# Stores of finished output tiles issued by SyncE in place of ScalarE, with a new table of priorities

## The chip, the cores and the metric

The kernel runs on one core of one Trainium2 chip. The metric is device time in microseconds (us) of one execution; lower is better. A core has TensorE (PE, with its weight loads shown apart as PEld), VectorE (DVE), ScalarE (ACT), GpSimd (POOL) and SyncE (SP). Each engine takes its own instructions in a fixed order and waits on semaphores for the others. In this program SP and ACT issue the transfers (DMAs) between HBM and the on-chip memory; everything that PE produces lies in eight PSUM banks until ACT or DVE copies it out.

## The reference

Two layers follow each other. The first is attention over 8 batches and 8 heads: 512 local tokens with a window of 32 tokens on either side, and 32 global tokens that see everything. The second takes its output as `x` (8 x 544 tokens that are kept, 512 wide), sends each token through the two best of four experts, and each expert is a causal attention with heads of 64.

```python
s_g  = scale * q_g @ k_all.T ; out_g = softmax(s_g) @ v_all            # 32 global tokens
s_l  = concat(scale * q_l @ k_g.T, where(|i-j|<=32, scale * q_l @ k_l.T, -1e9))
out_l = softmax(s_l) @ concat(v_g, v_l)                                # 512 local tokens
logits = x @ w_gate ; topk = two largest of 4 ; w = softmax over the two
for e in range(4):
    q, k, v = x @ wq[e], x @ wk[e], x @ wv[e]
    a = softmax(causal(scale * q @ k.T))
    out += (e in topk) * w[e] * (a @ v @ wo[e])
```

## The kernel before

The work is cut into steps. A step is one pair of heads of one batch of the first layer (32 pairs), and beside it a quarter of the second layer for a batch that is some steps behind. For one pair, `p1_load` and `p1_load_values` fetch `kn`, `qn` and `v` (line 407, SP), `p1_trans` turns them, `p1_scores` multiplies (32 calls that the profile shows as 64 matmuls, L681), `p1_softmax` runs on DVE and ACT (L693, L696), `p1_ptrans` turns the result (L714), `p1_av` multiplies with `v` (64 matmuls, L744). `long_scores` (L816, L824), `p1_global_av` (40 matmuls, L882) and `m_tail_av` (L1204) serve the global tokens. The second layer has `m_qk` (L912) and `m_v` (L943), 12 long matmuls each, `m_scores` (L1065), `m_softmax` (L1080 DVE, L1084 ACT, L1100 POOL), `m_ptrans` (turns, L714, then copies `ptu` and `ptl` out of PSUM), `m_av` (L1150) and the output.

The output is made by `out_tile`. It does six matmuls into a PSUM bank (L1223), has ACT copy the bank into an `ot` tile (L390; there are three `ot` buffers, which the loads of the next batch's global tokens use as well), and issues the store (L1230). `m_out` calls it for the four tiles of 128 tokens of a batch. Tiles 0 and 1 have their rows in mirrored groups and need four stores of 32 rows each; their stores go to SP. Tiles 2 and 3 need one store of 128 rows; their stores go to ACT. `m_out_tail` calls it once for batches 0 to 3 and once for batches 4 to 7, for the 32 global tokens of four batches at a time, with four stores of 32 rows; the first of these two goes to ACT by the default `via="ACT"`. The last batch and the second tail have `last` set, and either SP or ACT takes each of their stores.

The order is not written out by hand. Every piece of work is recorded by `op` with an estimated cost, and `Plan.place` then places all of them on the five engines by those estimates. Among what is ready on an engine the lowest `prio` goes first; `prio` is 100 per step plus small offsets. The table `SHIFT` (line 88) adds an offset of up to 150 to single pieces, found by kind, cost and step. So a changed table, or a piece on another engine, can change the order everywhere. What comes out is a fixed order per engine. Transfers report their landing on eight semaphores that the program uses in turn, for SP and ACT alike, in the order in which the planner emitted the transfers; before an issue the queue waits until the earlier transfer on the same semaphore has landed.

Of the kernel before, what the change touches and what calls it, by code (L numbers as in the profile page):

```python
# [49 lines left out]
class Op:  # L50
    def __init__(self, k, engs, ns, fn, prio, packets, shape, slow, code, flow):
# [34 lines left out]

OWN = 100
SHIFT = {
    "evac": {(180, 101): -100, (266, 110): 30, (276, 115): 100, (276, 123): 80, (369, 140): -110,
        (448, 103): 40, (475, 100): 130, (475, 102): 120, (475, 103): 90, (475, 106): 10, (475, 116): 80},  # L90
    "high_low": {(264, 125): 70, (332, 108): 100, (332, 109): -70, (332, 113): -50, (332, 114): 100,
        (332, 120): 20, (332, 125): 40, (477, 123): 30, (598, 119): 120, (598, 121): 70},
    "load": {(550, 104): 80, (550, 106): -10, (550, 108): -110, (550, 109): 100, (550, 111): 150,
        (550, 115): 110},
    "long_scores": {(60, 105): 80, (60, 129): -150, (60, 139): -110, (80, 115): -120, (80, 127): 10,
        (880, 103): -60, (880, 107): -70, (880, 109): -40, (880, 119): -40, (880, 125): -150, (880, 139): -120},
    "m_av": {(2220, 111): 30, (2220, 115): 90, (2220, 123): 40, (2220, 131): -10},
    "m_gates": {(350, 106): -40, (350, 123): -20, (630, 123): 140},
    "m_qk": {(1504, 107): 150, (1504, 112): -40, (1504, 124): 40, (1504, 136): 120},
    "m_scores": {(431, 110): 50, (431, 112): 50, (431, 116): 120, (431, 120): 90, (431, 124): 80,  # L100
# [3 lines left out]
    "m_softmax": {(80, 111): 60, (80, 119): 100, (211, 109): 80, (211, 121): -40, (344, 118): -90,  # L104
        (344, 126): -40, (344, 130): -70, (386, 131): -150, (386, 139): 50, (477, 109): -50, (477, 119): -90,
        (477, 125): 40, (599, 125): -70, (610, 108): 20, (644, 139): 20, (705, 114): 60},
    "m_tail_av": {(583, 113): -150, (583, 117): 40, (583, 125): 80, (583, 133): -90},
    "m_tail_factor": {(480, 123): 130},
    "m_tail_softmax": {(610, 119): -40, (745, 119): 30},
    "m_v": {(1440, 118): -40, (1440, 122): -30},  # L110
    "m_v_tails": {(330, 119): -150, (1062, 127): 90},
    "out_tile": {(450, 125): 70, (1400, 113): 90, (1400, 137): 150, (1400, 141): 150},
# [20 lines left out]
    "setup_masks": {(700, 105): 150},  # L133
    "turn_halves": {(250, 108): 20, (250, 109): -30, (250, 110): 120, (250, 118): -20, (250, 119): 20,
# [5 lines left out]
    "turned": {(84, 103): 150, (84, 109): 90, (84, 111): 10, (84, 113): 90, (84, 115): 100, (84, 123): 120,  # L140
        (220, 103): 140, (220, 113): -50, (255, 107): 90, (255, 113): 80, (255, 117): 120, (255, 131): 150},
}


# [193 lines left out]
def fused_kernel(ctx: ExitStack, tc: tile.TileContext, q_l, k_l, v_l, q_g, k_g, v_g,  # L338
# [552 lines left out]
    M = {}  # L891
# [158 lines left out]
    MIRRORED = (0, 1)  # L1050
# [161 lines left out]
                              ((lambda: y[0].t[:, :, b % 4, :], (y[0], b % 4)),  # L1212
                               (lambda: y[1].t[:, :, b % 4, :], (y[1], b % 4))), [(sm, 6)])

    def out_tile(y, lhs, dsts, via="ACT", last=False):

        hi, lo = weights["o"]
        po = ps([128, DM], "po")
# [14 lines left out]
    def m_out(b, i):  # L1233
        y = [(t, (c, n0)) for t in M[b, "yo"] for c in range(2) for n0 in ((0, 256) if b == B - 1 and c == 1 else (0,))
             if n0 == 0 and (i > 1 or n0 == 0 and not (b == B - 1 and c == 1)) or n0 == 256 and i < 2]
        at = Y_AT[i]
        if i in MIRRORED:
            dsts = [(out[b, 128 * i + 96 - 32 * g:128 * i + 128 - 32 * g, :], slice(32 * g, 32 * g + 32)) for g in range(4)]
        else:
            dsts = [(out[b, 128 * i:128 * i + 128, :], slice(0, 128))]  # L1240
        out_tile(y, lambda part, c: M[b, "yo"][part].t[:, c, at:at + 128], dsts, "SP" if i in MIRRORED else "ACT",
                 b == B - 1)

    def m_out_tail(g):
# [182 lines left out]
```

## Time and profile before

| | before |
|---|---|
| median of 3 runs | 467.47 us (467.24, 467.47, 469.96) |
| the profiled execution's own time | 469.88 us |
| its span, first to last instruction | 468.1 us |
| PE busy | 448.4 us (96%) |
| DVE, ACT, POOL busy | 377.2, 325.3, 289.8 us |
| stores of `ot` issued by SP, by ACT | 62, 26 |
| mean granted TensorE clock | 0.996 |

The profile is of one execution. Busy time is the union of an engine's instructions; a queue's waits and its issuing of transfers don't count as busy and are shown with a q (SPq, ACTq). A wait is put down to what ended last before it. The clock is given as a share of full speed: 1.0 is 2.4 GHz and 0.5 is 1.2 GHz.

### The profile page before, as it was taken

How to read it: one execution, taken by the hardware profiler on the slowest of the kernel's cores; microseconds unless marked ns; L12 is line 12 of the kernel's file. 1: busy time of each engine (PE TensorE's matmuls, PEld its weight loads, DVE VectorE, ACT ScalarE, POOL GpSimd, SP SyncE). 2: the span in 40 equal slices, each digit the busy share in tenths (PEclk: the TensorE clock that was granted, in tenths of full speed). 3: DMA queues.
4: the chain of work that ended last, by engine and by line, in shares of the span. 5: the costliest groups of instructions: out<-in, count | busy, mean ns of one | idle time of the engine just before them, and what ended most of it. 6: DMA issues, size and time to landing. Idle time of an engine off the chain costs nothing.

```text
span 468.1 us, 24864 instructions
## 1 busy us (share of the span) xinstructions
PE 448.4 (96%) x10124; PEld 389.1 (83%) x10124; DVE 377.2 (81%) x1689; ACT 325.3 (69%) x1166; POOL 289.8 (62%) x563
## 2 busy tenths in 40 slices
PE   8867999999999999999999999969999999999996
PEld 6656988897879988888979988858998899889875
DVE  6987899999887996789977997938977788568662
ACT  4886588886677776777766777937767666646481
POOL 8978878987987298722678693585849133232420
PEclk9999999999999999999999999999999999999999
DMA  8698566766526255432527424472022000200033
GB/s 179 136 188 150 110 121 118 154 104 119 100 56 144 50 110 105 114 65 49 107 44 171 88 54 71 107 153 64 5 56 74 22 4 3 63 32 1 4 92 113
DMA packets 182387, 40.95 MB, mean 87 GB/s; under 512 B 177664, under 2 KB 177664, under 8 KB 182272
## 3 DMA queue, kind: packets, MB, share of 16 engines
q1 hardware_dynamic: 179488, 34.51, 37.7%
q10 hardware_dynamic: 2784, 4.85, 3.0%
q8 instruction: 79, 1.29, 1.2%
q14 instruction: 36, 0.29, 0.2%
HBM read 30.42 MB, written 8.91 MB: 84 GB/s over the span
## 4 chain that ended last, share of the span: by engine, by line
PE 80%; DVE 7%; SPq 4%; issue 2%; ACT 2%; DMA 2%; POOL 1%; ACTq 0%; DVEq 0%; POOLq 0%
PE bank L912 17%; PE bank L1223 10%; PE bank L714 10%; PE bank L943 8%; PE bank L1150 8%; PE bank L1065 6%; PE bank L744 6%; PE bank L681 5%; SPq L407 4%; PE bank L816 2%; PE bank L882 2%; DVE st L693 1%; ACT st L696 1%; DMA msm<-in_moe_w_gate_dram 1%; PE bank L824 1%
## 5 line engine op out<-in xcount | busy, mean ns | idle before, releaser
L1100 POOL TENSOR_SCALAR pm<-pm,msm,gate 128x512 f32<-128x512 f32 (+3 forms) x124 | 75.0, 621 | 88.5 <-DVE msm L1089 31.8
L392 POOL COPY v<-v 32x512 f32<-32x512 f32 (+2 forms) x192 | 115.1, 600 | 23.5 <-DMA v<-in_v_l_dram 13.8
L696 ACT ACTIVATE st<-st,sm 128x128 f32<-128x128 f32 x256 | 99.7, 392 | 7.7 <-DVE sm L693 6.4
L1084 ACT ACTIVATE pm<-pm,msm 128x512 f32<-128x512 f32 (+3 forms) x128 | 70.8, 554 | 22.2 <-DVE msm L1080 21.8
L392 POOL COPY v<-vg 32x640 f32<-32x640 f32 (+1 forms) x96 | 66.1, 690 | 12.8 <-PE bank L882 5.8
L693 DVE CUSTOM_DVE_ANT_0 st<-bank,band 128x128 f32<-128x128 f32 x256 | 58.5, 284 | 1.8 <-PE bank L681 1.5
L696 ACT ACTIVATION_READ_ACCUMULATOR st<-st,sm 128x1 f32 x256 | 48.4, 189 | 0.0
L1065 PE MATMUL bank<-kt,qt 64*32 64x64 f32 (+15 forms) x1024 | 41.8, 405 | 3.9 <-ACT ptu L390 3.9
L390 ACT COPY ptu<-bank 128x512 f32<-128x512 f32 (+1 forms) x35 | 18.3, 543 | 38.2 <-PE bank L714 24.5
L681 PE MATMUL bank<-kd,qp 64*32 64x128 f32 x2048 | 40.1, 273 | 2.6 <-DVE qp L392 1.3
L1080 DVE CUSTOM_DVE_ANT_0 pm<-bank,cmask 128x512 f32<-128x512 f32 (+1 forms) x64 | 38.2, 618 | 3.6 <-PE bank L1065 2.1
L744 PE MATMUL bank<-v,ptw 128*32 128x64 f32 x2048 | 36.5, 220 | 4.7 <-issue 4.3
L744 PEld LDWEIGHTS bank<-v,ptw 128*32 128x32 f32 x2048 | 30.8, 110 | 10.1 <-issue 6.2
L681 PEld LDWEIGHTS bank<-kd,qp 64*32 64x32 f32 x2048 | 32.7, 105 | 7.3 <-issue 3.6
L912 PE MATMUL bank<-xh,wk_hi 128*128 128x272 f32 x128 | 38.3, 299 | 0.0
L912 PE MATMUL bank<-xh,wq_hi 128*128 128x272 f32 x128 | 37.0, 289 | 0.0
L912 PE MATMUL bank<-xl,wk_hi 128*128 128x272 f32 x128 | 36.9, 289 | 0.0
L912 PE MATMUL bank<-xh,wq_lo 128*128 128x272 f32 x128 | 36.9, 288 | 0.0
L912 PE MATMUL bank<-xl,wq_hi 128*128 128x272 f32 x128 | 36.9, 288 | 0.0
L912 PE MATMUL bank<-xh,wk_lo 128*128 128x272 f32 x128 | 36.9, 288 | 0.0
L943 PE MATMUL bank<-wv_hi,xh 128*128 128x260 f32 x128 | 36.8, 288 | 0.0
L943 PE MATMUL bank<-wv_lo,xh 128*128 128x260 f32 x128 | 36.2, 283 | 0.0
(184 smaller groups left out, 1308.6 us busy)
## 6 DMA issues: line engine op xcount, KB each, us to landing
v<-in_v_l_dram SPq DMA_DIRECT2D x64, 120.0 KB, 3.0
kn<-in_k_l_dram SPq DMA_DIRECT2D x104, 64.0 KB, 2.8
qn<-in_q_l_dram SPq DMA_DIRECT2D x104, 64.0 KB, 2.5
out_dram<-ot ACTq DMA_DIRECT2D x16, 256.0 KB, 2.4
out_dram<-ot SPq DMA_DIRECT2D x62, 64.0 KB, 1.8
v<-in_v_l_dram SPq DMA_DIRECT2D x32, 64.0 KB, 2.9
kn<-in_k_l_dram SPq DMA_DIRECT2D x12, 128.0 KB, 3.3
qn<-in_q_l_dram SPq DMA_DIRECT2D x12, 128.0 KB, 3.2
```

The source lines that it names most:

```text
L392: ENG[e].tensor_copy(out, in_)
L681: nc.tensor.matmul(sp[h].t[32 * g:32 * g + 32, 128 * t:128 * t + 128], qp.t[rows, 32 * u:32 * u + 32], kd.t[rows, c:c + 128], start=True, ...
L693: op("DVE", 211, lambda e, h=h, t=t, i=i: nc.vector.tensor_tensor_reduce(out=st.t[:, h, t], in0=sp[h].t[:, 128 * t:128 * t + 128], in1=ban ...
L696: op("ACT", 385, lambda e, h=h, t=t, i=i: nc.scalar.activation(st.t[:, h, t], st.t[:, h, t], AF.Exp, bias=sm.t[:, 0, i:i + 1], scale=-1.0, ...
L714: nc.tensor.transpose(two[y].t[:, k, :], block()[rows], ident[rows, rows])
L744: nc.tensor.matmul(xq.t[32 * g:32 * g + 32, t, h, :], pt.t[:, h, 32 * u:32 * u + 32], v.t[:, h, window(u), :], start=True, stop=True)
L912: nc.tensor.matmul(pp.t, w[:, ch, cols], x(part, ch)[:, n], start=(ch == 0 and w is hi and part == 0), stop=(ch == NCH - 1 and part == 1))
L943: nc.tensor.matmul(pv.t, x(part, ch)[:, 128 * i:128 * i + 128], w[:, ch, :], start=(ch == 0 and part == 0 and w is hi), stop=(ch == NCH - ...
L1065: nc.tensor.matmul(sp[x].t[32 * g:32 * g + 32, at:at + n], qt.t[rows, q0:q0 + 32], kt.t[rows, :n], start=True, stop=True)
L1084: op("ACT", 280 + 0.83 * n, lambda e, x=x, at=at, n=n, s=s: nc.scalar.activation(pm.t[:, x, at:at + n], pm.t[:, x, at:at + n], AF.Exp, bia ...
L1100: lambda e, x=x, at=at, n=n, row=row, s=s: ENG[e].tensor_scalar(pm.t[:, x, at:at + n], pm.t[:, x, at:at + n], sm.t[:, 3, s:s + 1], gate.t[ ...
L1223: nc.tensor.matmul(po.t, lhs(part, c), w[:, c, :], start=(c == 0 and part == 0 and w is hi), stop=(c == 1 and part == 1))
```

## The change

`out_tile` gets `via="SP"` as its default, and `m_out` passes "SP" for all four tiles. So 18 stores that ACT issued (the two 128-row stores of batches 0 to 6, and the four 32-row stores of the first tail) are issued by SP; SP then has 80 stores and ACT 8. The stores with `last` set are as before. The table `SHIFT` is replaced by another one, which moves pieces on every engine. Three lines are added above, so each line after the table stands three further down. The arithmetic, the tiles and the buffers stay.

```diff
 SHIFT = {
-    "evac": {(180, 101): -100, (266, 110): 30, (276, 115): 100, (276, 123): 80, (369, 140): -110,
+    "evac": {(180, 100): -90, (180, 101): -20, (276, 111): 50, (316, 102): -40, (316, 104): 90,
...
@@
-    def out_tile(y, lhs, dsts, via="ACT", last=False):
+    def out_tile(y, lhs, dsts, via="SP", last=False):
...
-        out_tile(y, lambda part, c: M[b, "yo"][part].t[:, c, at:at + 128], dsts, "SP" if i in MIRRORED else "ACT",
+        out_tile(y, lambda part, c: M[b, "yo"][part].t[:, c, at:at + 128], dsts, "SP",
                  b == B - 1)
```

The rows below show three places; all three stand around the end of batch 3, where the first tail's output is stored. First ACT. Before, from the copy of batch 3's last `ot` tile on (`yth` is the first half of the tail's input, `vt`, `ptu`, `ptl`, `longt` are copies of PSUM banks, `xh` is the first layer's turned output):

```order
L390 COPY ot<-bank_68 128x512
L390 COPY ptw<-bank_64 128x8x64
L780 CAST xh<-bank_66 64x2x32 x2
L780 CAST yth<-bank_67 64x2x32 x2
L1230 DMA out_dram<-ot 128x512
L390 COPY vt<-bank_70 128x260
L696 ACTIVATE st,sm<-st,sm 128x128 x6
L390 COPY ot<-bank_68 128x512
L1230 DMA out_dram<-ot 32x512 x4
L390 COPY ptu<-bank_66 128x2x3x64
L390 COPY ptl<-bank_67 128x6x64
L401 CAST xh<-bank_69 128x4x64
```

And ACT at the same place after the change:

```order
L393 COPY ot<-bank_64 128x512
L699 ACTIVATE st,sm<-st,sm 128x128 x3
L783 CAST xh<-bank_67 64x2x32 x2
L783 CAST yth<-bank_71 64x2x32 x2
L393 COPY ptw<-bank_69 128x8x64
L852 ACTIVATE long,sgm<-long,sgm 128x544
L393 COPY ot<-bank_68 128x512
L393 COPY longt<-bank_69 128x5x64
L393 COPY ptu<-bank_71 128x2x3x64
L393 COPY ptl<-bank_64 128x6x64
```

The five stores (one of 128 rows, four of 32) are gone from between the copies: the tail's `ot` copy is followed at once by the copies of `longt`, `ptu` and `ptl`.

Second SP. Before, from batch 3's eight 32-row stores on (`v`, `qn`, `kn`, `vg` are loads for later steps):

```order
L1230 DMA out_dram<-ot 32x512 x8
L407 DMA v<-in_v_l_dram 96x5x64 x2
L407 DMA v<-in_v_l_dram 128x2x64
L407 DMA v<-in_v_l_dram 96x5x64 x2
L407 DMA v<-in_v_l_dram 128x2x64
L407 DMA qn<-in_q_l_dram 32x16x32 x4
L407 DMA kn<-in_k_l_dram 32x16x32 x4
L407 DMA qn<-in_q_l_dram 32x16x32 x4
L407 DMA vg<-in_v_g_dram 32x8x64
```

And SP after the change, from the third and fourth tile of batch 3 to the tail's four stores:

```order
L1233 DMA out_dram<-ot 128x512
L410 DMA kn<-in_k_l_dram 32x16x32
L410 DMA v<-in_v_l_dram 96x5x64 x2
L1233 DMA out_dram<-ot 128x512
L410 DMA v<-in_v_l_dram 128x2x64
L410 DMA v<-in_v_l_dram 96x5x64 x2
L410 DMA v<-in_v_l_dram 128x2x64
L410 DMA kn<-in_k_l_dram 32x16x32 x2
L410 DMA qn<-in_q_l_dram 32x16x32 x4
L410 DMA kn<-in_k_l_dram 32x16x32 x3
L1233 DMA out_dram<-ot 32x512 x4
L410 DMA kn<-in_k_l_dram 32x16x32
```

The stores now stand between the loads of one queue: a store that waits for its `ot` copy holds the loads behind it.

Third PE, one step later. Before, `p1_av` (L744) and `p1_global_av` (L882) follow `m_scores`, then come `m_av` (L1150) and turns, and `p1_scores` comes after those:

```order
L1065 MATMUL bank_71<-kt,qt 32x32
L744 MATMUL bank_69<-v,ptw 32x64 x32
L882 MATMUL bank_68<-v,longt 32x64 x20
L1150 MATMUL bank_66<-ptl,vt 64x256 x2
L1150 MATMUL bank_66<-ptl,vt 64x128 x2
L1150 MATMUL bank_66<-ptu,vt 64x256 x6
L1150 MATMUL bank_66<-ptu,vt 64x128 x2
L714 MATMUL bank_67<-ident,st 128x64
```

After the change `m_av` (L1153) stands ahead, and the last of the 32 calls of `p1_scores` (L684) are followed by `p1_av` and `p1_global_av`, then by `m_qk` (L915). Each call shown here is two matmuls in the profile for L684, L747 and L885:

```order
L684 MATMUL bank_70<-kd_77,qp 32x128
L684 MATMUL bank_68<-kd_77,qp 32x128
L747 MATMUL bank_65<-v,ptw 32x64 x32
L885 MATMUL bank_71<-v,longt 32x64 x20
L915 MATMUL bank_67<-xh,wk_hi 128x272
L915 MATMUL bank_67<-xh,wk_lo 128x272
```

So three pieces of many short matmuls (64, 64 and 40 in the profile) now stand in a row.

## Rows read from the trace of the kernel before

**Rows 1.** The page: busy us (share of the span) and instructions of each engine.

```profile
PE 448.4 (96%) x10124; PEld 389.1 (83%) x10124; DVE 377.2 (81%) x1689; ACT 325.3 (69%) x1166; POOL 289.8 (62%) x563
```

**Rows 2.** Windows: stretch, length, busy us (x instructions) of PE, PEld, DVE, ACT, POOL; clock, DMA, GB/s.

```profile
0.00:47.00 47.00, 36.45 (x996) 28.78 (x997) 37.77 (x173) 32.96 (x122) 39.90 (x91) 1.00 0.80 163
47.00:311.30 264.30, 262.83 (x6254) 231.97 (x6252) 229.78 (x1043) 195.79 (x724) 185.71 (x348) 1.00 0.51 100
311.30:315.30 4.00, 0.05 (x6) 0.03 (x4) 0.55 (x2) 0.56 (x2) 3.49 (x7) 0.90 0.70 133
315.30:318.70 3.40, 3.40 (x73) 2.26 (x77) 2.08 (x9) 1.77 (x5) 0.00 (x0) 0.61 0.29 58
```

**Rows 3.** Waits of PE: who waited for whom, us in total, times, longest.

```profile
PE bank L744 <- issue: 4.3, 4, 1.4
PE bank L1065 <- ACT ptu L390: 3.9, 1, 3.9
```

**Rows 4.** The chain that ended last, from 305 to 320 us: start, us, what.

```profile
310.21 1.71 SPq L407
...
312.27 2.03 DMA kn<-in_k_l_dram
...
314.33 0.32 ACTq L1230
...
315.28 3.35 PE bank L1065 x54
```

**Rows 5.** Timeline of ACT: start, us, engine, line, operation, tiles [idle before, releaser].

```profile
309.99 4.66 ACTq L1230 DMA_DIRECT2D out_dram<-ot  x4
314.74 0.48 ACT L390 COPY ptu<-bank 128x384 f32<-128x384 f32 x1 [7.11 <-DMA out_dram<-ot]
```

**Rows 6.** Timeline of SP's queue at the same place.

```profile
307.10 2.01 SPq L407 DMA_DIRECT2D qn<-in_q_l_dram  x4
309.22 3.36 SPq L407 DMA_DIRECT2D kn<-in_k_l_dram  x4
```

**Rows 7.** Timeline of PE: `m_scores` behind the wait, and the same 64 matmuls elsewhere.

```profile
315.28 3.35 PE L1065 MATMUL bank<-kt,qt 64*32 64x416 f32 x64 [3.95 <-ACT ptu L390]
...
428.76 2.07 PE L1065 MATMUL bank<-kt,qt 64*32 64x416 f32 x64
```

**Rows 8.** Line 1230, the stores: duration ns min/median/max, first and last start us.

```profile
L1230 SPq DMA_DIRECT2D out_dram<-ot x62: 314/423/1446, 140.2 to 462.8; - x62
L1230 ACTq DMA_DIRECT2D out_dram<-ot x26: 321/357/483, 140.7 to 465.2; - x26
```

**Rows 9.** Waits of SP's queue.

```profile
SPq L1230 <- ACT ot L390: 110.3, 7, 43.5
```

**Rows 10.** Timeline of PE in the first 47 us: `p1_av` with waits put down to issue.

```profile
35.29 0.66 PE L744 MATMUL bank<-v,ptw 128*32 128x64 f32 x33 [1.41 <-issue]
...
38.15 1.09 PE L744 MATMUL bank<-v,ptw 128*32 128x64 f32 x61
40.59 0.25 PE L744 MATMUL bank<-v,ptw 128*32 128x64 f32 x2 [1.35 <-issue]
```

**Rows 11.** The page: DMA queue, kind: packets, MB, share of 16 engines.

```profile
q8 instruction: 79, 1.29, 1.2%
```

**Rows 12.** Timeline of PE: three short-matmul pieces in a row without a wait.

```profile
344.75 0.77 PE L882 MATMUL bank<-v,longt 128*32 128x64 f32 x40
345.34 1.07 PE L744 MATMUL bank<-v,ptw 128*32 128x64 f32 x64
346.23 0.74 PE L1204 MATMUL bank<-vt,longt 128*32 128x64 f32 x40
```

**Rows 13.** The tile kn: its loads and its first reader; ns min/median/max, first and last start us.

```profile
L407 SPq DMA_DIRECT2D kn<-in_k_l_dram x116: 311/487/2010, 1.6 to 312.3; - x116
L661 DVE STREAM_TRANSPOSE kd<-kn x26: 618/670/679, 46.4 to 355.7; 128x480 f32<-128x480 f32 x26
```

**Rows 14.** Waits of ACT for a store's landing at an `ot` copy.

```profile
ACT ot L390 <- DMA out_dram<-ot: 1.6, 2, 1.2
```

More of the change, by code (lines that the diff above doesn't have):

```diff
@@ L88 @@
 SHIFT = {
-    "evac": {(180, 101): -100, (266, 110): 30, (276, 115): 100, (276, 123): 80, (369, 140): -110,
[L90 to L100, printed above, removed]
[3 rows of a table removed]
@@ L104 @@
[L104 to L110, printed above, removed]
@@ L111 @@
-    "m_v_tails": {(330, 119): -150, (1062, 127): 90},
-    "out_tile": {(450, 125): 70, (1400, 113): 90, (1400, 137): 150, (1400, 141): 150},
[20 rows of a table removed]
-    "setup_masks": {(700, 105): 150},
-    "turn_halves": {(250, 108): 20, (250, 109): -30, (250, 110): 120, (250, 118): -20, (250, 119): 20,
[5 rows of a table removed]
-    "turned": {(84, 103): 150, (84, 109): 90, (84, 111): 10, (84, 113): 90, (84, 115): 100, (84, 123): 120,
-        (220, 103): 140, (220, 113): -50, (255, 107): 90, (255, 113): 80, (255, 117): 120, (255, 131): 150},
+    "evac": {(180, 100): -90, (180, 101): -20, (276, 111): 50, (316, 102): -40, (316, 104): 90,
+        (448, 101): -130, (475, 100): 150, (475, 104): 50, (475, 107): 120, (475, 113): 140, (475, 123): -10},
@@ new lines @@
+    "high_low": {(332, 114): -150, (332, 119): -110, (332, 122): -120, (332, 123): -60, (598, 119): 50},
+    "load": {(550, 103): 150, (550, 104): 150, (550, 105): 110, (550, 106): 100, (550, 107): 120,
+        (550, 109): 140, (550, 110): 150},
+    "long_scores": {(60, 105): 120, (60, 117): -100, (60, 121): -40, (60, 129): -120, (60, 139): -150,
+        (80, 111): -150, (80, 127): -30, (80, 131): -30, (880, 107): -60, (880, 109): -90, (880, 113): 30,
+        (880, 115): -80, (880, 119): -100, (880, 127): -100, (880, 131): -30, (880, 139): -70},
@@ new lines @@
+    "m_av": {(2220, 111): 40, (2220, 117): -20, (2220, 119): -140, (2220, 121): -90, (2220, 123): 100,
+        (2220, 125): -70, (2220, 127): -90, (2220, 129): -20, (2220, 131): -70, (2220, 133): -50},
+    "m_gates": {(630, 119): -100, (950, 115): 120},
+    "m_qk": {(1504, 107): 120, (1504, 124): 50, (1504, 131): -20, (1504, 136): 140},
+    "m_scores": {(431, 108): -20, (431, 110): 50, (431, 114): -40, (431, 116): 70, (431, 118): -50,
[4 rows of a table added]
+    "m_softmax": {(80, 119): 10, (211, 109): -150, (211, 115): -60, (211, 119): -70, (211, 123): -40,
+        (211, 127): 20, (386, 139): 150, (431, 139): -120, (477, 111): -30, (477, 125): 50, (477, 127): 150,
+        (599, 119): 150, (610, 110): -10, (705, 108): -20, (705, 132): 110},
@@ new lines @@
+    "m_tail_av": {(583, 113): 60},
+    "m_tail_softmax": {(100, 119): -80, (110, 127): 90, (610, 111): -50, (610, 127): -120, (745, 115): 40},
+    "m_v": {(300, 126): 20, (1440, 118): -100, (1440, 122): -120, (1440, 126): -130, (1440, 130): -60},
+    "m_v_tails": {(1062, 119): -50, (1062, 127): 100},
+    "out_tile": {(1400, 137): 150},
[19 rows of a table added]
+    "setup": {(163, 102): -60, (1000, 109): 60, (1165, 102): 100},
+    "setup_masks": {(700, 105): 50},
+    "turn_halves": {(250, 102): -110, (250, 110): 80, (250, 111): 50, (250, 112): 30, (250, 115): 20,
[7 rows of a table added]
@@ L142 @@
+    "turned": {(84, 109): 100, (84, 113): 70, (84, 115): 80, (84, 121): -10, (84, 123): 140, (84, 125): -40,
+        (220, 113): -80, (220, 119): 120, (255, 127): -130},
 }
```

58 rows, old and new, of the table SHIFT are left out of this document.

## Prediction, written before the changed kernel ran

> **What bounds the kernel now.** I read the page first, then the windows, the waits of PE, the chain of waits, and the timelines at the one place to which these point. The page says that PE is busy for 448.4 of 468.1 us [rows 1]; no other engine is near that. The windows say where the missing time lies. In the first 47 us PE works 36.45 us, so 10.55 are lost while the pipeline fills. From 47 to 311.3 us it works 262.83 of 264.30 us: in those 264 us nothing that another engine does better can win more than 1.5 us. From 311.3 to 315.3 us it does nothing at all, 0.05 of 4.00 us, and in the 3.4 us behind that it is busy but at a granted clock of 0.61 [rows 2]. So outside the start and the last store there is one hole, and the first thing to learn is who made it.
>
> The waits of PE name it: `m_scores` (L1065) waited 3.9 us, once, for ACT's copy of `ptu` out of its PSUM bank [rows 3]. ACT was not working at that time. Its copy of `ptu` began 7.11 us late, put down to the landing of stores, and just ahead of it stand the four stores of the first tail, which ACT's queue issued from 309.99 on over 4.66 us [rows 5], though one issue takes 0.36 [rows 8]. The chain of waits shows what they waited for: SP's queue at 310.21 with a load that took 1.71 us to issue, then the flight of `kn`, 2.03 us, then ACT's last store at 314.33, then PE at 315.28 [rows 4]. The stores share their landing semaphores with the loads that SP was issuing at that time, four `qn` and four `kn` from 307.10 on [rows 6]. So ACT's in-order queue stood behind SP's loads, the PSUM copies stood behind ACT's stores, and PE behind the copies.
>
> **The change part by part.** *The 18 stores leave ACT.* What this removes at 311 us: the wait, 3.95 us, and the slow stretch behind it. The 64 matmuls of `m_scores` took 3.35 us there, and the same 64 took 2.07 us at 428.76 us [rows 7]. The difference, 1.28 us, is the price of the lower clock, which fell to its level of 1.2 GHz after PE had stood still. Together 5.23 us. For this to come back, ACT must find no other reason to be late there. In the new order its copies of `longt`, `ptu` and `ptl` follow the tail's `ot` copy without a store between, so what ACT can wait for is PE itself and a free `ot` buffer.
>
> The Trainium skill (DMA: Bandwidth & Descriptors, "Issuing engines are not separate DMA queues") says that issuing from several engines only saves sequencer time. By that rule the move would be worth ACT's issue time alone; the trace has more than that in it, because an issue that waits stops the engine's copies too.
>
> That issue time by itself is 18 x 0.357 = 6.4 us of ACT [rows 8]. I cost it at nothing: ACT is idle for 468.1 - 325.3 = 142.8 us [rows 1], and PE is full where the other stores stand, so the 1.5 us of idle time between 47 and 311 us is the most that could come of it. If ACT were the bound it would be a gain of 6.4.
>
> *The 18 stores arrive on SP.* They cost 18 x 0.423 = 7.6 us of issue [rows 8], and hold up the loads behind them. I cost that at nothing as well. SP stood for 110.3 us in front of stores whose `ot` was not yet there [rows 9], and still the loads were early: the last `kn` load is issued at 312.3 us and the last `kn` is first read at 355.7 us [rows 13]. Uncovered it would be a loss of up to 7.6.
>
> *The new order on PE.* The same pieces run, so the sum of matmul time is the same. What can differ is how they are packed. The profile shows waits put down to "issue", 4.3 us of them in `p1_av` alone [rows 3]. PE's program is loaded in packets while it runs: 79 packets on the instruction queue [rows 11], and 10124 matmuls with 10124 weight loads [rows 1] make 20248 / 79 = 256 instructions, or 128 matmuls, for each. Between the wait that ends at 35.29 us and the one that ends at 40.59 us lie 5.30 us [rows 10]. I take such a wait to be a packet that came late because short matmuls use up 128 in less time than a packet needs. After the change `p1_scores`, `p1_av` and `p1_global_av` stand in a row one step behind the tail, 64 + 64 + 40 = 168 short matmuls where before 64 + 40 stood together. Bounds: below, nothing, since 40 + 64 + 40 = 144 short matmuls ran in a row at 344.75 us without a wait [rows 12]; above, two waits as at 35.29 us, 2 x 1.41 = 2.8 us. The case is longer than the one that passed and is a `p1_av` as the ones that waited, so I take one wait, 1.4 us.
>
> The other reorderings, among them some at the start, I cost at nothing, with 1.4 us either way for one such wait more or less [rows 10].
>
> *The sum.* Against the profiled execution's own time: 469.88 - 5.23 + 1.4 = 466.05 us. That execution lies 2.41 us above the median of 467.47; one of the three runs lies as high and two do not. If the 2.41 us have nothing to do with the hole, the median falls by the whole 3.83 us, to 463.64. If they are the hole itself, which is then shorter in a median run, the median keeps 2.41 of the gain and becomes 466.05. Nothing in one profile decides this, so I take the middle, **464.8 us**.
>
> **The rivals.** *Nothing is given back.* The packed matmuls cost nothing and the hole closes in full: 467.47 - 5.23 = 462.2 us. For it speaks that the 144 in a row passed [rows 12], and that a DMA share of 0.80 in the first 47 us [rows 2], which may have slowed the packets, is not everywhere. Against it, that at the end of batch 3 the share is high as well (0.70 in the hole).
>
> *The hole stays.* At the same place ACT's copies may still be late, behind the `ot` copy of the tail, which needs the landing of an earlier tile's store from a queue that is now shared with the loads. Then the 5.23 us stay, the packing costs its 1.4, and the time is 468.9 us. For it: two `ot` copies waited for a landing before, 1.6 us in total [rows 14]. Against it: those waits were short, and the tail's copy comes well after the batch's own four.
>
> *SP becomes the limit.* If every one of the 18 issues fell on the path, 463.6 + 7.6 = 471.2 us. The Trainium skill (Perfetto Trace Analysis, "DMA Optimizations") advises to spread DMAs over the issuing engines where issuing is what limits; by it this change goes the wrong way. Against this rival stand SP's 110.3 us of waiting for stores [rows 9] and the 43 us of lead of the last `kn` load [rows 13].
>
> *Slower: the ring of three `ot` buffers.* A batch's third and fourth tile are now stored behind eight 32-row issues and some loads, up to 12 issues or 12 x 0.423 = 5.1 us later than on ACT's own queue. If the next user of the buffer is an ACT copy that finds it taken, ACT stands, and the PSUM copies behind it. The hole gives the rate: ACT stood 7.11 us and PE lost 3.95 of it [rows 5, 7], so about 3.2 us are covered. A wait of 5.1 us at each of the seven batch ends would cost 7 x 1.9 = 13.3 us and give 463.6 + 13.3 = 476.9 us. It decides, that is, the time passes 472.1, where the wait passes 3.2 + 8.5 / 7 = 4.4 us. Against it: the fourth tile's copy needs the first tile's buffer, whose store stands first in SP's queue now as before.
>
> **How the numbers follow.** About 1% is what a measurement of this kernel can tell from no change: 4.7 us, so faster means under 462.8 and slower over 472.1. Forecast (463.6 to 466.1 with its own bounds of 1.4 either way): 0.50. Nothing given back: 0.20. The hole stays: 0.15. SP the limit: 0.05. The ring: 0.10. Faster is nearly all of the second case and the low edge of the first, 0.19 + 0.07 = 0.26. Slower is the ring and the top of SP's case, 0.09 + 0.02 = 0.11. The same is the rest, 0.63. For the range I go from 461.5, just under the second case, to 470.0, above the case in which the hole stays; below lie about 0.07, above about 0.13.
>
> **What would show it.** Right: no wait of PE for ACT's copy of `ptu` around the tail's output, and the clock at 1.0 throughout; a wait put down to issue of 1 to 2 us in L747 or L885 right behind L684, one step on; no ACT wait for a landing of stores but in the last batch; the loads still ahead of their readers. Wrong: a hole of some us in the windows after 47 us at another place; ACT waiting for stores at `ot` copies at each batch's end; DVE or POOL waiting for loads after the first 135 us. The forecast falls if the median of before never had the whole hole, or if the start of the program, where the order of PE also changes, moves by more than the one wait that I allow.

## The result and the profile after

On one chip, in 14 runs each, the kernel before took 469.85 us in the median (466.88 to 473.98) and the changed kernel 464.96 us (461.60 to 467.52): a ratio of 0.990, with a 95% interval from 0.987 to 0.993. Ratios, here and below, compare the means of the fast runs, so that the few slow runs count in the medians but not in the ratios. The profiled execution of after took 462.31 us and lies 2.65 us under its own median, so its total is not set against the 469.88 us of before; what follows is read place by place.

The page of after: busy us and share of the span of each engine, then the queues on which SP's (q1) and ACT's (q10) transfers ran, with packets, MB and share.

```profile
PE 445.9 (97%) x10124; PEld 388.0 (84%) x10124; DVE 375.1 (81%) x1686; ACT 325.5 (71%) x1169; POOL 292.6 (64%) x563
...
q1 hardware_dynamic: 181696, 38.44, 40.5%
...
q10 hardware_dynamic: 576, 0.92, 0.7%
```

PE has the same 10124 matmuls as in [rows 1]; ACT's queue keeps 576 packets, those of the last batch and the second tail. The windows of after, with the columns of [rows 2], in stretches cut for its own time axis:

```profile
0.00:47.00 47.00, 38.63 (x1015) 31.61 (x1016) 39.55 (x179) 34.99 (x136) 42.18 (x91) 0.96 0.77 162
47.00:300.00 253.00, 250.68 (x6141) 221.07 (x6141) 219.41 (x1017) 191.94 (x706) 179.41 (x337) 1.00 0.50 99
300.00:320.00 20.00, 20.00 (x419) 17.36 (x419) 16.21 (x75) 13.13 (x49) 14.32 (x25) 1.00 0.60 124
```

Where before had 4 us of nothing and then 3.4 us at a clock of 0.61, the 20 us around the first tail are now full, at a clock of 1.00. PE's waits of after, by total (us in total, times, longest):

```profile
PE bank L717 <- DVE xn L751: 2.8, 2, 2.5
PE bank L747 <- issue: 2.0, 3, 0.9
PE bank L1383 <- DVE pm L1378: 1.4, 1, 1.4
PE bank L684 <- ACT qp L393: 1.0, 1, 1.0
```

The wait for ACT's copy of `ptu` [rows 3] is gone and nothing of its size took its place. The longest, 2.5 us for `xn`, lies in the filling pipeline at 35.82 us. The timeline of ACT after, at the tail, from the copy of the tail's `ot` on:

```profile
306.74 0.59 ACT L393 COPY ot<-bank 128x512 f32<-128x512 f32 x1 [4.41 <-issue]
307.23 0.43 ACT L393 COPY longt<-bank 128x320 f32<-128x320 f32 x1
307.54 0.50 ACT L393 COPY ptu<-bank 128x384 f32<-128x384 f32 x1
307.91 0.51 ACT L393 COPY ptl<-bank 128x384 f32<-128x384 f32 x1
```

Four copies follow each other without a wait (the view puts the 4.41 us ahead of the first down to issue; they end 0.08 us after PE's last matmul for that tile), where [rows 5] had 7.11 us between the `ot` copy and `ptu`. The four stores are now SP's; they take 3.14 us there, against 4.66 on ACT, and next behind them on SP stands a load:

```profile
307.99 3.14 SPq L1233 DMA_DIRECT2D out_dram<-ot  x4
311.18 0.43 SPq L410 DMA_DIRECT2D kn<-in_k_l_dram  x1
```

And PE after, at the same place and one step on, `m_scores` first:

```profile
308.05 2.15 PE L1068 MATMUL bank<-kt,qt 64*32 64x416 f32 x63
...
313.48 1.14 PE L684 MATMUL bank<-kd,qp 64*32 64x128 f32 x61
...
314.55 1.10 PE L747 MATMUL bank<-v,ptw 128*32 128x64 f32 x64
315.46 0.74 PE L885 MATMUL bank<-v,longt 128*32 128x64 f32 x40
```

`m_scores` starts without a wait and takes 2.15 us, not the 3.35 of [rows 7]. The three pieces of short matmuls run in a row without a wait for their code; the term of 1.4 us that the prediction put here did not appear.

### The profile page after: what moved, and what is told of

It is laid out like the page before. It is cut to its first block, busy times and chain, and to the rows that moved or that the text cites. A ratio compares the mean times of both kernels' runs of the same rounds, so it can differ in the third digit from the quotient of the medians.

```text
span 460.5 us, 24884 instructions
## 1 busy us (share of the span) xinstructions
PE 445.9 (97%) x10124; PEld 388.0 (84%) x10124; DVE 375.1 (81%) x1686; ACT 325.5 (71%) x1169; POOL 292.6 (64%) x563
## 4 chain that ended last, share of the span: by engine, by line
PE 75%; SPq 8%; POOL 5%; DMA 5%; DVE 3%; issue 2%; ACT 1%; POOLq 0%; DVEq 0%
PE bank L915 16%; PE bank L1226 10%; PE bank L717 9%; PE bank L1153 8%; SPq L410 8%; PE bank L946 8%; PE bank L1068 7%; PE bank L684 5%; PE bank L747 5%; POOL v L395 4%; DMA v<-in_v_l_dram 2%; PE bank L819 2%; PE bank L885 2%; DMA pm<-in_moe_wo_dram 1%; PE bank L963 1%
## 5 line engine op out<-in xcount | busy, mean ns | idle before, releaser
L395 POOL COPY v<-v 32x512 f32<-32x512 f32 (+2 forms) x192 | 116.6, 607 | 23.3 <-DMA v<-in_v_l_dram 13.9
L1087 ACT ACTIVATE pm<-pm,msm 128x128 f32<-128x128 f32 (+3 forms) x128 | 70.7, 554 | 23.8 <-DVE msm L1083 23.5
L395 POOL COPY v<-vg 32x640 f32<-32x640 f32 (+1 forms) x96 | 67.1, 700 | 19.9 <-PE bank L885 7.4
L684 PE MATMUL bank<-kd,qp 64*32 64x128 f32 x2048 | 39.1, 272 | 1.2 <-ACT qp L393 1.0
L747 PE MATMUL bank<-v,ptw 128*32 128x64 f32 x2048 | 36.7, 223 | 2.0 <-issue 2.0
L915 PE MATMUL bank<-xh,wk_hi 128*128 128x272 f32 x128 | 38.5, 301 | 0.0
L1068 PE MATMUL bank<-kt,qt 64*32 64x96 f32 (+15 forms) x1024 | 38.5, 394 | 0.0
L684 PEld LDWEIGHTS bank<-kd,qp 64*32 64x32 f32 x2048 | 32.7, 105 | 5.3 <-issue 2.2
L915 PE MATMUL bank<-xh,wq_hi 128*128 128x272 f32 x128 | 37.1, 290 | 0.0
L915 PE MATMUL bank<-xl,wk_hi 128*128 128x272 f32 x128 | 36.9, 289 | 0.0
L915 PE MATMUL bank<-xl,wq_hi 128*128 128x272 f32 x128 | 36.9, 288 | 0.0
L915 PE MATMUL bank<-xh,wq_lo 128*128 128x272 f32 x128 | 36.9, 288 | 0.0
L915 PE MATMUL bank<-xh,wk_lo 128*128 128x272 f32 x128 | 36.9, 288 | 0.0
L747 PEld LDWEIGHTS bank<-v,ptw 128*32 128x32 f32 x2048 | 31.3, 112 | 6.4 <-issue 2.8
L946 PE MATMUL bank<-wv_hi,xl 128*128 128x260 f32 x128 | 36.1, 282 | 0.0
```

What stands on the lines that cost most here:

```text
L395: ENG[e].tensor_copy(out, in_)
L684: nc.tensor.matmul(sp[h].t[32 * g:32 * g + 32, 128 * t:128 * t + 128], qp.t[rows, 32 * u:32 * u + 32], kd.t[rows, c:c + 128], start=True, ...
L747: nc.tensor.matmul(xq.t[32 * g:32 * g + 32, t, h, :], pt.t[:, h, 32 * u:32 * u + 32], v.t[:, h, window(u), :], start=True, stop=True)
L915: nc.tensor.matmul(pp.t, w[:, ch, cols], x(part, ch)[:, n], start=(ch == 0 and w is hi and part == 0), stop=(ch == NCH - 1 and part == 1))
L946: nc.tensor.matmul(pv.t, x(part, ch)[:, 128 * i:128 * i + 128], w[:, ch, :], start=(ch == 0 and part == 0 and w is hi), stop=(ch == NCH - ...
L1068: nc.tensor.matmul(sp[x].t[32 * g:32 * g + 32, at:at + n], qt.t[rows, q0:q0 + 32], kt.t[rows, :n], start=True, stop=True)
```

## Experiments

Twelve runs in three groups; each group ran on one chip beside runs of the kernel before. The first group is e1 to e4, the second after again, e3 again, e7 and e8, the third e1 again, e5, e9 and e10. Medians of that group's before: 468.26, 468.33 and 467.94 us. "Order kept" means that every engine's sequence of computing instructions stays; only the stores change their queue or place.

| run | what differs | median us | ratio to before, 95% interval |
|---|---|---|---|
| e1 | before, 18 stores on SP | 464.88 | 0.992 (0.989 to 0.995) |
| e1, again | the same | 463.54 | 0.991 (0.988 to 0.994) |
| e3 | before, only the tail's four on SP | 462.36 | 0.988 (0.984 to 0.993) |
| e3, again | the same | 462.32 | 0.987 (0.984 to 0.991) |
| e4 | before, only the fourteen single ones on SP | 469.08 | 1.001 (0.998 to 1.004) |
| e7 | before, tail's four on ACT, behind the copies | 464.71 | 0.992 (0.989 to 0.995) |
| e8 | before, tail's output as one store, on ACT | 463.47 | 0.990 (0.987 to 0.994) |
| e9 | before, as two stores, on ACT | 466.83 | 0.995 (0.992 to 0.998) |
| after, again | the changed kernel | 464.83 | 0.992 (0.989 to 0.995) |
| e2 | after, 18 stores back on ACT | 464.88 | 0.994 (0.991 to 0.996) |
| e10 | after, the fourteen back on ACT | 465.26 | 0.996 (0.993 to 0.998) |
| e5 | stores on SP, old table, order planned anew | 465.11 | 0.993 (0.990 to 0.996) |

The theory: the hole at 311 us is made by the tail's four stores standing in ACT's queue ahead of the copies, and they stand because their landing semaphores are shared with loads of SP. The rivals: the new order brings the gain; the fourteen single stores bring it; ACT is late for another reason.

### The issue alone, and the order alone

e1 keeps the order of before and moves the issuing of all 18; e2 keeps the order of after and gives the 18 back to ACT.

```diff
 # e1, on the kernel before
-... lambda e, dst=dst, rows=rows: ENG[e].dma_start(dst, ot.t[rows]), ...
+... lambda e, dst=dst, rows=rows: ENG[e if last else "SP"].dma_start(dst, ot.t[rows]), ...
 # e2, on the kernel after; m_out passes acts = i not in MIRRORED
+... ENG[e if last or not acts else "ACT"].dma_start(dst, ot.t[rows]), ...
```

> The order of before is kept on every engine, instruction by instruction; only the 18 issues of stores that ACT made are made by SP instead, at the place in SP's queue at which the old plan emitted them. Theory (the hole at 311 us comes from ACT's queue standing in front of stores): the wait of PE for the copy of ptu is gone or under 1 us, no clock below full speed behind it, and the ratio to before is about 0.989 (5.2 of 470 us less). Rival 1 (the new table makes the gain, not the issuing queue): ratio 1.000 within 0.003, with the hole still there or its time lost elsewhere. Rival 2 (SP becomes the limit, or the ring of three ot buffers): ratio over 1.005, with ACT waiting for landings of stores at ot copies or DVE and POOL waiting for loads after 135 us.

> The order of the changed kernel is kept on every engine; only the 18 issues of stores go back to ACT's queue, at the place at which the new plan emitted them. Theory (the issuing queue makes the gain): ACT stands in front of the tail's four stores for some us again, PE waits for a copy behind it, and the ratio to before is 0.998 to 1.003. Rival (the new order makes the gain): ratio 0.990 as the changed kernel, no hole.

e1 took 464.88 us, with no hole: the windows of e1 around the tail read

```profile
305.00:320.00 15.00, 15.00 (x358) 12.91 (x362) 10.04 (x37) 10.84 (x39) 11.79 (x20) 1.00 0.67 142
```

So the issue alone brings the gain; the table isn't needed for it. e2 has no hole either, at 464.88 us, though ACT issues the stores again. That is not what the theory expected of e2 (a hole, 0.998 to 1.003) but what its rival did. The timeline of ACT in e2 says why:

```profile
310.58 0.59 ACT L393 COPY ot<-bank 128x512 f32<-128x512 f32 x1 [4.06 <-PE bank L1226]
311.07 0.43 ACT L393 COPY longt<-bank 128x320 f32<-128x320 f32 x1
311.20 0.34 ACTq L1233 DMA_DIRECT2D out_dram<-ot  x1
311.64 0.48 ACT L393 COPY ptu<-bank 128x384 f32<-128x384 f32 x1
312.01 0.49 ACT L393 COPY ptl<-bank 128x384 f32<-128x384 f32 x1
...
314.24 0.32 ACTq L1233 DMA_DIRECT2D out_dram<-ot  x1
314.60 0.72 ACT L1087 ACTIVATE pm<-pm,msm 128x512 f32<-128x512 f32 x1 [1.55 <-DMA kn<-in_k_l_dram]
```

In the new order the stores come out spread over the copies instead of ahead of all of them, because the planner placed them on another queue. The last one still waits for a load of `kn`, but only after `ptu` and `ptl` are done. Either half of the change alone takes the hole away, and the halves don't add.

### Which of the 18 stores

e3 moves only the four 32-row stores of the first tail, e4 only the fourteen stores of 128 rows.

```diff
 # e3
+... ENG["SP" if len(dsts) == 4 and not last else e].dma_start(dst, ot.t[rows]), ...
 # e4
+... ENG["SP" if len(dsts) == 1 and not last else e].dma_start(dst, ot.t[rows]), ...
```

> The order of before is kept; only the four 32-row stores of the first tail are issued by SP. Theory (the four stores of the tail alone made the hole): ratio about 0.989, as with all 18. Rival (the fourteen single stores cost as much, by 0.4 us of issue each and short waits): ratio 0.995 or above here, and the rest in the run that moves those fourteen.

> The order of before is kept; the fourteen 128-row stores are issued by SP, the four stores of the first tail stay on ACT. Theory (the tail's four make the hole, and 14 x 0.36 us of ACT's issue time are covered): ratio 1.000 within 0.003, the hole of about 4 us at 311 us still there. Rival: ratio 0.995 or below, the hole gone or smaller because SP and ACT are then at other places.

e3 took 462.36 us and e4 469.08. In e3 the window around the tail is full:

```profile
305.00:320.00 15.00, 15.00 (x351) 12.91 (x354) 9.98 (x37) 10.81 (x39) 11.86 (x20) 1.00 0.62 125
```

In e4 the hole stands unchanged, as its waits show (us in total, times, longest), and its window around the tail:

```profile
ACT ptu L390 <- DMA out_dram<-ot: 7.1, 1, 7.1
...
PE bank L1065 <- ACT ptu L390: 4.0, 1, 4.0
```

```profile
305.00:320.00 15.00, 11.01 (x242) 8.76 (x241) 7.26 (x28) 5.92 (x19) 7.64 (x14) 0.77 0.50 100
```

Four stores carry the whole gain; the fourteen carry nothing while the hole stands.

### What the four stores wait for

e7 leaves the four on ACT but puts them into its queue behind the copies of `ptu`, `ptl`, `xh` and `longt`.

```diff
 # in copy(): nc.scalar.copy(out, in_), flush()
+...     hold(len(dsts) == 4 and not last and e == "ACT", lambda: ENG[e].dma_start(dst, ot.t[rows])), ...
+    held, past = [], []
+    def hold(wait, go): held.append(go) if wait else go()
+    def flush(): past.extend([1] * bool(held)), [held.pop(0)() for _ in list(held) if len(past) == 3]
```

> The kernel before, with the first tail's four stores still on ACT but put into its queue behind the copies of ptu, ptl, xh and longt. Theory (only what stands behind the waiting stores in ACT's queue makes the hole): ACT may still wait some us for landings, but with nothing behind that PE needs at once; no wait of PE for ptu over 0.5 us, the clock stays at 1.0, 4 to 5 us less than before. Rival (ACT is late at this place for another reason, the tail's own ot copy or its matmuls): the wait of PE for ptu stays over 2 us and the time within 2 us of before.

464.71 us, 3.6 less than before, where 4 to 5 were expected; `m_scores` does not wait for the copy of `ptu`. The timeline of ACT in e7 shows `ptu` waiting for PE, not for a store:

```profile
309.35 0.59 ACT L390 COPY ot<-bank 128x512 f32<-128x512 f32 x1
312.77 0.48 ACT L390 COPY ptu<-bank 128x384 f32<-128x384 f32 x1 [2.83 <-PE bank L714]
...
314.04 0.47 ACT L390 COPY longt<-bank 128x320 f32<-128x320 f32 x1
314.96 1.46 ACTq L1230 DMA_DIRECT2D out_dram<-ot  x3
```

So ACT is not late for another reason. Between the end of the `ot` copy and the point where `ptu` can start lie 2.83 us in which ACT has nothing to do anyway. Put later, the four stores come onto other semaphores too, those of the four `kn` loads; these landed at 314.89 to 315.58 us, after the copies, so that ahead of the copies the stores would have held ACT here as well.

e8 makes the four stores one store of 128 rows, e9 makes them two of 64 rows, both on ACT ahead of the copies as before.

```diff
 # e8: only the first of the four placed pieces issues
+            ENG[e].dma_start(out[0:4, SL:, :], ot.t[:, :])
 # e9: the first and the third
+            ENG[e].dma_start(out[g:g + 2, SL:, :], ot.t[32 * g:32 * g + 64])
```

> The kernel before, with the first tail's four stores of 32 rows made one store of 128 rows, on ACT, ahead of the copies as before. In the order of emission it stands where the first of the four stood, and the transfer eight places ahead of it is one of ACT's own stores, long landed; the second to fourth stood behind loads of SP on their semaphores. Theory (the shared landing semaphores make the wait): ACT's queue spends under 0.6 us at this place instead of 4.66, the wait of 3.9 us and the slow stretch are gone, 4 to 5 us less than before. Rival (the number of issues is what costs): three issues less, 3 x 0.36 = 1.1 us of the hole go and some 2.9 us of wait stay.

> The kernel before, with the first tail's four stores of 32 rows made two of 64 rows, on ACT, at the same place of its queue. In the built program the one store of the run before waits for the second of the four qn loads; two stores wait for the second and the fourth of the four qn loads; the four stores of the kernel before wait for these two and for the second and the fourth of the four kn loads. Theory (ACT stands until the load on its last store's semaphore has landed): the fourth qn load is issued two places, some 1.0 us, behind the second, so ACT's copy of ptu begins about 3.2 + 1.0 to 1.4 = 4.2 to 4.6 us late, PE waits 0.7 to 1.7 us for it instead of 3.95, and the time is 3 to 4 us below before. Rival (a store more costs its issue alone): 3.2 + 0.4 us, no wait of PE.

The premise written for e8 was wrong: the store does not follow one of ACT's own. The built program of before lists what each issue waits for. The eight semaphores, 0 to 7, go round over both queues; the tail's stores and the loads ahead of them wait for

```
SP   qn  L407   semaphores 6, 0, 1, 2
SP   kn  L407   semaphores 3, 4, 5, 6
ACT  ot  L1230  semaphores 0, 2, 4, 6   (the tail's four stores)
SP   qn  L407   semaphores 7, 1, 3, 5   (between the stores)
```

The first store thus waits for the landing of the second `qn` load, the second for the fourth `qn`, the third and fourth for the second and fourth `kn`. The trace of before bears this out: these four loads landed at 309.92, 312.61, 313.03 and 314.31 us, and the four stores were issued at 309.99, 312.63, 313.06 and 314.33. e8's one store has semaphore 0, e9's two have 0 and 2. The timelines of ACT and of SP in e8, and behind them the line on flights from the view of the tile `qn` from 303 to 309 us:

```profile
304.46 0.59 ACT L390 COPY ot<-bank 128x512 f32<-128x512 f32 x1
306.97 1.14 ACTq L1251 DMA_DIRECT2D out_dram<-ot  x1
308.21 0.48 ACT L390 COPY ptu<-bank 128x384 f32<-128x384 f32 x1 [3.16 <-DMA out_dram<-ot]
```

```profile
304.15 2.00 SPq L407 DMA_DIRECT2D qn<-in_q_l_dram  x4
```

```profile
DMA to landing us min/median/max: 2.2/2.2/2.3
```

SP issues the four `qn` loads over 2.00 us from 304.15, so the second at about 304.65; 2.2 to 2.3 us later, at about 306.9, it has landed, and at 306.97 ACT's store is issued. (The landing of the second load itself is not in the view; 2.2 to 2.3 us are those of its neighbours.) The issue took 1.14 us, not the under 0.6 that was expected. ACT stood for 3.16 us, PE for none, and the time is 463.47 us, without the hole.

The timelines of ACT and of PE in e9, and between them two pieces of the chain that ended last from 303 to 316 us:

```profile
308.37 3.40 ACTq L1251 DMA_DIRECT2D out_dram<-ot  x2
311.87 0.48 ACT L390 COPY ptu<-bank 128x384 f32<-128x384 f32 x1 [5.74 <-DMA qn<-in_q_l_dram]
```

```profile
307.03 4.19 DMA qn<-in_q_l_dram
...
311.25 0.53 ACTq L1251
```

```profile
312.40 3.10 PE L1065 MATMUL bank<-kt,qt 64*32 64x416 f32 x64 [2.56 <-ACT ptu L390]
```

Two issues alone take 0.7 us [rows 8], these took 3.40, and the trace names the load of `qn` as what ended ACT's wait. The expected size was missed, 5.74 us on ACT against 4.2 to 4.6: the fourth `qn` load, on which the second store waited, landed 4.2 us after its issue at 307.03, not 2.0 to 2.3 as those ahead of it did. PE lost 2.56 us instead of 0.7 to 1.7, and the time is 466.83 us, 1.1 below before in the median (2.3 by the ratio) instead of 3 to 4. The mechanism held: the store was issued 0.02 us after that load had landed, and the time lies between the kernel before and the ones without a hole. Put together, ACT's standing and PE's loss are

| kernel | tail's stores on ACT | ACT stands | PE waits | difference |
|---|---|---|---|---|
| e8 | one | 3.16 | 0 | - |
| e9 | two | 5.74 | 2.56 | 3.18 |
| before, e4 | four | 7.11, 7.11 | 3.95, 4.0 | 3.16, 3.1 |

About 3.2 us are free, and behind that each us costs PE one. One run was not made: the four stores left in their place ahead of the copies, but on semaphores of their own. That the shared semaphores make the wait rests on the landing times of before and e9 and on the table of the built program.

### The order and the fourteen, again

> The changed kernel once more, now on the same chip as kernels of the old order. Theory (the gain is the hole at the first tail and nothing else): about 0.990 of before, 4 to 5 us less, and equal within 1.5 us to the kernel that only issues the tail's four stores from SP. Rival (the new order is worth something of its own, for instance at the place where short matmuls stand in a row): over 2 us away from that kernel, to either side.

> The kernel before with only the first tail's four stores issued by SP, again, for comparison on one chip with the changed kernel. Theory: 0.988 to 0.992 of before, the same as the changed kernel within 1.5 us. Rival (new order better or worse by itself): over 2 us apart.

The changed kernel took 464.83 us, e3 462.32, with intervals of the ratio that touch (0.989 to 0.995, 0.984 to 0.991). The expectation was a distance of at most 1.5 us; at 2.5 us it is the rival's mark, over 2 us, that was reached. The distance could be the order, the fourteen stores, or spread. Two more kernels on one chip were to take these apart; e10 gives the fourteen back to ACT in the new order.

```diff
 # e10, on the kernel after
+... ENG["ACT" if len(dsts) == 1 and not last else e].dma_start(dst, ot.t[rows]), ...
```

> The kernel before with all 18 stores issued by SP, order kept, again. Question: whether the fourteen single stores cost something on SP when the hole is gone. If they do, about 464.9 us, 2.5 us above the kernel that moves only the tail's four (462.3 to 462.4 us twice). If that distance was spread between runs: 462 to 463.5 us.

> The changed kernel with the fourteen single stores given back to ACT, the tail's four left on SP, order kept. If the fourteen on SP cost about 2.5 us: 462.3 us, and this is the best version of the new order. If they cost nothing: as the changed kernel, 464.8 to 465.0 us, and what separates the two orders is the order.

e1 came out at 463.54 us and e10 at 465.26. If the fourteen cost something on SP, e10 would have been the faster, so in the new order they cost nothing that shows. By what was written for e10, this leaves the order. Whether it is the order can be read from pairs with equal issuing, and the two pairs do not agree:

| issued by SP | old order, ratio to before | new order, ratio to before |
|---|---|---|
| all 18 | e1: 0.992, 0.991 | after: 0.990, 0.992 |
| the tail's four | e3: 0.988 (0.984 to 0.993), 0.987 (0.984 to 0.991) | e10: 0.996 (0.993 to 0.998) |

With all 18 on SP these runs can tell no difference. With the four alone the new order is some 0.8% slower, and the intervals do not overlap; but e3 and e10 ran on different chips, each beside its own runs of before. So the rival that the new order costs some us of its own has not fallen. e3 had the lowest median of all, twice, and no cause is claimed for its distance to after.

### The old table with the stores planned on SP

Here the two edits of `via` are made without the new table.

> The kernel before with the 18 stores on SP for the planner too, and the old table of priorities, so that the whole order is planned anew with numbers that were found for another plan. Theory (the hole is the only thing the stores make, and no copy of ptu stands behind a store): no hole at the first tail, 4 to 5 us less than before, if the new plan has no hole of its own. Rival (the table is as much of the change as the stores): waits of PE of some us at other places, and a time of 467 us or more.

465.11 us, 2.8 less than before where 4 to 5 were expected, and no hole: in ACT's timeline at the tail `ptu` again waits only for PE.

```profile
310.92 0.59 ACT L390 COPY ot<-bank 128x512 f32<-128x512 f32 x1 [0.59 <-ACT st L696]
314.30 0.48 ACT L390 COPY ptu<-bank 128x384 f32<-128x384 f32 x1 [2.79 <-PE bank L714]
```

The rival (waits of PE of some us elsewhere, 467 us or more) has fallen: the hole goes without the new table.

## Why the prediction was right

The forecast was 464.8 us and the median came out at 464.96. The mechanism, the hole at the tail, was right; that the number came so close is in part luck, as the terms show. Its terms one by one:

**The hole, 5.23 us: right in place and cause, less sure in size.** Wait and slow stretch are both gone in after. e3 and e4 show that the tail's four stores make them, e7 that it is their place ahead of the copies, e8 and e9 that it is the loads on the shared semaphores. As a share, 5.23 of 469.88 us is a ratio of 0.989; the five measurements of kernels that have the old order and no hole (e1 and e3 twice each, e7) lie from 0.987 to 0.992, and e8 at 0.990. In us these medians lie 3.4 to 6.0 below before, and the changed kernel's 4.9 and 3.5, so 5.23 is one profile's figure and not a median's. Nor is the whole hole in every run: one run of before, at 464.87 us, and one of e4, at 465.83, have a mean granted clock of 1.0 over the whole run, which does not leave room for a slow stretch as in [rows 2].

**ACT's and SP's issue time at nothing: right as far as the runs can tell.** The fourteen stores alone moved nothing (e4, 1.001). The waits on SP in front of stores are nearly as long as before: after has `SPq L1233 <- ACT ot L393` with 101.5 us, where [rows 9] has 110.3. PE waited for a `kn` load twice for 0.8 us together, in the first 47 us, and for no load after that. One sign that the prediction named for being wrong did come: after 135 us POOL waited 9.9 us for `v` loads in after, 6.4 in before. It cost PE little or nothing: all of PE's waits after 47 us come to 2.2 us, the longest 0.8 and put down to issue. The Trainium skill (DMA: Bandwidth & Descriptors, "Issuing engines are not separate DMA queues") says that issuing from several engines only saves sequencer time. The ratio of e4, 1.001, agrees with that for the fourteen stores; for the four it leaves out what cost 5.23 us in the profile of before, that an issue which waits holds its engine's next copies.

**The dense place, 1.4 us: wrong, it measured 0.** In after 61 + 64 + 40 recorded short matmuls ran at 313.48 us without a wait, and none of the other profiles of the new order (after again, e2, e10) shows a wait put down to issue between 305 and 320 us. The bound from below, 144 in a row without a wait [rows 12], was the right end to take: it stood in the same dense part of the program, while the waits of 1.41 and 1.35 us [rows 10] come from the first 47 us. `p1_av`'s waits put down to issue went from 4.3 to 2.0 us in after's profile, and stand at 0.25 to 0.94 each. That a late packet of the program makes them stays an inference that no run tested: the page of before has two instruction queues, with 79 and 36 packets, and names the engine of neither. The other reorderings, too, were costed at nothing; by e10 against e3 that is open.

**Own time or median: the middle was wrong too.** The prediction held open whether the 2.41 us by which the profiled execution lay above the median of three had to do with the hole, and took half. With 14 runs the median of before is 469.85 us: on that chip the profiled 469.88 was an ordinary run, and the median of three was a low one. So the plain sum there was 469.88 - 5.23 = 464.65 us, 0.31 under what was measured. The forecast came to 464.8 because it added 1.4 that was not there and took off 1.2 because it put half of the 2.41 us down to a profiled run above the ordinary: two errors that cancel. On the chips of the experiments the medians of before were 467.94 to 468.33; after again, at 464.83, lay 1.7 us above its group's 468.33 - 5.23 = 463.1. So an agreement within 0.2 us is more than the terms can carry.

**The rivals.** "The hole stays" and "SP becomes the limit" fell with after's windows. The ring of three `ot` buffers did show itself, once. ACT's timeline in after, at the end of batch 1:

```profile
193.49 0.59 ACT L393 COPY ot<-bank 128x512 f32<-128x512 f32 x1 [4.57 <-DMA out_dram<-ot]
195.47 0.59 ACT L393 COPY ot<-bank 128x512 f32<-128x512 f32 x1 [1.39 <-DMA out_dram<-ot]
```

And SP at that place, then the windows around it:

```profile
187.32 2.85 SPq L410 DMA_DIRECT2D kn<-in_k_l_dram  x4
190.27 3.72 SPq L1233 DMA_DIRECT2D out_dram<-ot  x8
```

```profile
190.00:193.00 3.00, 3.00 (x24) 2.86 (x23) 0.43 (x1) 0.00 (x0) 2.84 (x7) 1.00 0.61 133
193.00:196.00 3.00, 3.00 (x28) 3.00 (x26) 0.86 (x2) 1.12 (x2) 2.87 (x5) 1.00 0.62 156
```

SP's eight stores stand behind four loads, ACT waits 4.57 us for a buffer, near the 5.1 that the rival had, and PE is busy for 6.00 of these 6.00 us at a clock of 1.00. The price was 0: PE had long matmuls to do and waited for nothing there. It happened at one batch end of seven. The prediction's sign that ACT would wait for no store but in the last batch was wrong, and the clock was not at 1.0 throughout either (0.96 in the first 47 us).

What stays open: why e3 is 2.5 us below after, if it is, and whether the new order gives back at another place some of what the hole brings.

## What to carry to other kernels

An issue is an instruction of its engine, and where landings are counted on a few semaphores that go round over all queues, it can wait for a transfer of another queue that has nothing to do with it. So look at what stands behind an issue on its engine: put stores behind the copies that the bounding engine needs, issue them from an engine that computes nothing, or make one store of four. And look at when a load lands and when the store on its semaphore is issued: the two times show such a wait at once. And before a distance between a profiled run and a median of three is built into a forecast, count how many runs that median has.

## What the runs showed that was not expected

The first 47 us differ from run to run with the same program. Kernels e7 and e8 are the kernel before up to 300 us; the first window of before [rows 2], of e7 and of e8:

```profile
0.00:47.00 47.00, 37.65 (x1002) 29.50 (x1003) 38.06 (x179) 33.38 (x126) 41.73 (x93) 0.96 0.77 163
```

```profile
0.00:47.00 47.00, 39.36 (x1014) 31.83 (x1015) 39.13 (x181) 34.77 (x133) 42.50 (x94) 0.96 0.79 164
```

The mean granted clock was 1.00 in before and 0.96 in these two, and PE had started 996, 1002 and 1014 matmuls by then. So a 0.96 in the first window comes without the new order too. But the new order has it far more often: its four profiles have 0.96 three times and 0.93 (e2), and of the 50 runs of after, after again, e2 and e10 one has a mean granted clock of 0.998 or more over the whole run; of the 47 runs of e1, e3, e7 and e8, which have the old order and no hole, 29 do. What decides it was not tested, nor what it costs; some of the spread of some 1% between runs may come from there.

A transfer's flight is as uneven: the loads of `qn` ahead of the tail landed in 2.2 to 2.3 us in e8 and in 2.0 to 4.2 us in e9, and through the shared semaphore that came out as a wait of PE.
